# Second group's second layer partly in three passes, half of the h tiles scaled in place in PSUM, and another order of the w_out parts

## The chip, the cores and the metric

One Trainium2 chip, of which one core is used. A core has a tensor engine (PE; its weight loads are shown apart, as PEld), a vector engine (DVE), a scalar engine (ACT), a gpsimd engine (POOL) and a sync engine (SP), which here issues every DMA in program order. The metric is the device time of one execution in microseconds (us); times are the median of several runs. Each engine runs its own queue of instructions in order and waits on semaphores where it needs another engine's result. PSUM, into which PE writes, has eight banks here, all handed out from one pool.

## The reference

A gated linear attention feeds a two-layer network. q, k, v and alpha have 4 batches, 8 heads, 768 steps and 48 channels.

```
for t in range(S):
    state = alpha[t][:, None] * state + outer(k[t], v[t])     # 48 x 48 per head
    y[t] = q[t] @ state
x = y with batch and step as 3072 rows, head and channel as 384 columns
h = maximum(x @ w_in, 0)          # w_in 384 x 2048
out = (h * h) @ w_out             # w_out 2048 x 384, out 3072 x 384 in fp32
```

w_in and w_out arrive as 64-bit floats and are turned into fp32 on DVE and ACT at the start.

## The kernel before, in words

**Tiles.** The sequence is cut into chunks of 128 steps: 6 chunks times 4 batches are 24 blocks. Four blocks, one chunk of all batches, are a group of 512 tokens; there are 6 groups, 0 to 5. The hidden size of 2048 is 16 tiles of h, each 128 x 512 (hidden channels by the group's tokens). Each weight matrix is cut into 8 pieces of 128 x 768, two tiles of h each.

**Order.** The program is written under a manual schedule: each engine runs its instructions in the order in which the Python code gives them. The attention of group g + 1 is woven into the network of group g. `weave` (L885) walks a list of units of the network, each with a cost (one unit is about 1.3 us of PE), and ahead of each unit it puts the events whose position has come. Events are attention steps, preparation of weights, splits of x, and loads. Their positions stand in the dictionary `AT` (L19) and in `PLAN` and `EARLY`.

**Two ways to multiply.** A plain fp32 product runs as two records on PE. In the other way, three passes in the faster fp32r type, each factor is split into a rounded part and a rest: `cast_w` (L561) makes b of a weight piece on ACT, `rest_w` (L565) the rest l on DVE, `scale_w` (L569) scales l by 1/E on ACT (E is 2^-12), and `diff_w` (L574) makes d, the difference of b and l, on DVE. `split_to` and `diff_to` make a, l and d of x or h: a on ACT (L600), l on DVE (L559), d on DVE (L604). A product is then E times the sum of b·a and l·l, plus d·d. The l and d parts of all pieces are stored to DRAM by `scale_w` and `diff_w` and loaded back into SBUF when room comes free: `pump` (L589) issues the next load of a list as long as fewer than `room` parts are held, and `stream(g)` puts the next group's list there at unit 26. The tiles for weights come from one pool of 25 (`wt_pool`).

**Groups.** Group 0 computes both layers plain (`ffn_in` L758, `ffn_out` L778 with its products at L783). Group 1 computes layer 1 in three passes and layer 2 plain. Groups 2 to 5 use three passes in both. While group 1 runs, the rest of w_in (pieces 4 to 7) and all of w_out are prepared for the groups behind it.

**Layer 1 in three passes** (`layer_in`). `in_x` (L634) gives the b·a and l·l products of an h tile (L626), and ACT copies the bank to an SBUF tile with the factor E (L639). Two tiles later `in_y` (L641) gives the d·d products in the same bank, and DVE adds them to the SBUF tile (L559). At `AT["post"]`, four tiles later, `in_post` (L645) takes max(h, 0) squared: odd tiles in one DVE operation (L648), even tiles in two ACT operations (L652, L653).

**Layer 2 in three passes** (`layer_out`). A first sweep over the 16 tiles, `out_x` (L697), adds the a·b and l·l products of four token tiles into four banks (L692); ACT copies them to SBUF with E. A second sweep, `out_y` (L714), adds the d·d products, DVE adds the two, and the rows are stored. `split_h` and `diff_h` make the parts of h ahead of that.

**Attention, per block.** Logarithms of alpha are summed along the chunk by a product with a triangular matrix, `cs` (L273). Blocks below `SPLIT`, 8, do it in one plain product (L278); others have their logarithms split on DVE (`sp`, L269 and L270) and use two fp32r products (L281, L282). Exponentials of the sums scale q and k; `turn` (L486) transposes both into two banks (L494); `ga` and `gb` then give scores (L389), sums of k times v for each half of the chunk (`state_sums`, L406, products L413), the new state (`sums_copied` L420, `next_state` L427 on DVE) and y (L365). The k·v sums are 64 columns wide, of which 16 are a neighbouring head's and are not used.

Of the kernel before, what the change touches and what calls it, by code (L numbers as in the profile page):

```python
# [18 lines left out]
AT = {'evs': 0.8, 'lead': 4, 'post': 4, 'w_first': (40, 44, 48, 52), 'wstep': 1, 'w_in_at': 2, 'w_in_by': 3.4, 'w_out_at': 27, 'w_out_by': 3.6, 'room1': 6, 'room': 9, 's0': 2, 'ahead': 5, 'late': 1, 'xs': 0.5, 'g1': (2.7, 20, 32.0), 'g': (1.2, 15.5), 'g1x': 48, 'gx': 46, 'g0x': 55.5, 'pre': 0, 'ga': 9, 'gb': 12}  # L19

# [6 lines left out]
def kernel(  # L27
# [10 lines left out]

# [27 lines left out]
    s_t = [p2.tile([128, NP, 64], FP32, tag="s", name="s", bufs=B + 2) for _ in range(B)]  # L78
    for t in s_t:
        nc.gpsimd.memset(t, 0.0)  # L80
    NV = 4
# [8 lines left out]
    wt_pool = ctx.enter_context(tc.tile_pool(name="wt", bufs=25))  # L90
# [13 lines left out]

# [39 lines left out]


# [75 lines left out]
    for i in range(2):  # L221
        rows = slice(64 * i, 64 * (i + 1))
        nc.gpsimd.tensor_copy(out=halves_mask[rows], in_=causal[rows, rows])
    last = consts.tile([128, 4, NP], FP32, name="last")
# [36 lines left out]
    SPLIT = 2 * GB  # L261
# [113 lines left out]

# [27 lines left out]
    def state_sums(n):  # L406
        ps = two[n]
        for p in range(NP):
            for e in range(2):
                first = (2 * p + e) * D - G * e  # L410

                for h in range(1 if n // B == NCH - 1 else 2):
                    nc.tensor.matmul(  # L413
                        out=ps[h][64 * e : 64 * (e + 1), 1, p, :],
                        lhsT=tile_of("k", n)[HALF[h], 2 * p + e, :],
                        rhs=tiles["v"][n % NV][HALF[h], first : first + 64],
                        start=True, stop=True, skip_group_check=True,
                    )

    def sums_copied(n):  # L420

        ps = two.pop(n)
        u = blk[n]["u"] = p2.tile([128, NP, 64], FP32, tag="us", name="us", bufs=3)
        nc.vector.tensor_tensor(out=u, in0=ps[0][:, 1], in1=s_t[n % B], op=ALU.add)
        blk[n]["kv1"] = ps[1][:, 1]

    def next_state(n):  # L427
        blk[n]["s"] = s_t[n % B]
        if n // B < NCH - 1:
            s = s_t[n % B] = p2.tile([128, NP, 64], FP32, tag="s", name="s", bufs=B + 2)  # L430
            last = last_t[n % 4].unsqueeze(2).to_broadcast([128, NP, 64])
            nc.vector.tensor_tensor(out=s, in0=blk[n].pop("kv1"), in1=blk[n]["u"], op=ALU.add)
            nc.vector.tensor_tensor(out=s, in0=s, in1=last, op=ALU.mult)
# [18 lines left out]
    def ga(a, n):  # L452

        if n is not None:
            for f in (scores, state_sums, masked, sums_copied):
                f(n)
        if a is not None:
            product = y_begin(a)
            for h in range(1 if a < B else 0, 2):
                for m, p, e in heads(a):  # L460
                    rows = slice(64 * e, 64 * e + D)
                    s = blk[m]["u" if h else "s"]
                    product(m, p, e, s[rows, p, 0 : D + G * e], blk[m]["qs"][rows, p, HALF[h]], HALF[h])


            for m, p, e in heads(a):
                end = inner(product, m, p, e, e)
            passed = nc.gpsimd.nop(nofuse=True)
            dep(passed, end)
            two["y"] = product, passed  # L470
        if n is not None:
            next_state(n)
# [79 lines left out]
    here, todo, room = {}, [], [6]  # L552
# [11 lines left out]

    def rest_w(w, p):  # L565
        l = here["l", w, p] = wt("wl", FP32R, shapes[w])
        combine(((l, whole[w][p], ALU.subtract, here["b", w, p].bitcast(FP32)),))

    def scale_w(w, p):  # L569
        l = here["l", w, p]  # L570
        nc.scalar.activation(out=l, in_=l.bitcast(FP32), func=AF.Copy, scale=1.0 / E)
        nc.sync.dma_start(out=kept_parts["l", w, p], in_=words(l))

    def diff_w(w, p):  # L574
        b, l = (here[x, w, p].bitcast(FP32) for x in "bl")
        d = here["d", w, p] = wt("wd", FP32R, shapes[w])
        combine(((d, b, ALU.subtract, l),))
        nc.sync.dma_start(out=kept_parts["d", w, p], in_=words(d))
        if w == "o":
            here.pop(("l", w, p))  # L580
            here.pop(("d", w, p))
            pump()
# [6 lines left out]
    def pump():  # L589
        while todo and sum(k[0] in "ld" for k in here) < room[0]:  # L590
            key = todo.pop(0)
            here[key] = wt("w" + key[0], FP32R, shapes[key[1]])
            nc.sync.dma_start(out=words(here[key]), in_=kept_parts[key])
# [40 lines left out]
    def in_x(j):  # L634
# [3 lines left out]
        hid[j] = two_k("hid")  # L638
        nc.scalar.activation(out=hid[j], in_=acc["h", j], func=AF.Copy, scale=E)  # L639

    def in_y(j):  # L641
        in_passes(j, "d", "d", False, True)
        combine(((hid[j], acc.pop(("h", j)), ALU.add, hid[j]),))

    def in_post(j):  # L645
        h = hid[j]
        if j % 2:
            nc.vector.scalar_tensor_tensor(  # L648
                out=h, in0=h, scalar=0.0, in1=h, op0=ALU.max, op1=ALU.mult
            )  # L650
        else:
            nc.scalar.activation(out=h, in_=h, func=AF.Relu)  # L652
# [5 lines left out]
    def layer_in(g):  # L658
        units = []
        for n in range(NJ + 2):  # L660
# [6 lines left out]
            if g > 1 and AT["lead"] <= n < AT["lead"] + AHEAD:  # L667
                units.append((0, split_h, (n - AT["lead"],)))
                units.append((0, diff_h, (n - AT["lead"],)))
# [5 lines left out]
    def split_h(n):  # L675
        r = n % (AHEAD + MORE)
        if r < AHEAD:
            a, l = two_k("ha", FP32R), two_k("hl", FP32R)
        else:
            if n < AHEAD + MORE and r == AHEAD:  # L680
                extra[:] = [raw_r("hx") for _ in range(3)]
            i = 2 * (r - AHEAD)
            a, l = (extra[i // 3][:, i % 3] for i in (i, i + 1))
# [6 lines left out]

    def of_tile(t, lhs, rhs, start=False, stop=False):
# [5 lines left out]
    def out_x(n):  # L697
        p, jj = divmod(n, 2)
        a, l = h_parts.pop(n)
        for t in range(GB):  # L700
            if n == 0:
                acc[t] = ps_ffn.tile([128, GB * C], FP32, tag="att", name="o")
            of_tile(t, a, here["b", "o", p][:, jj], start=n == 0)
            of_tile(t, l, here["l", "o", p][:, jj], stop=n == NJ - 1)
            if n == NJ - 1:
                if t % 2 == 0:
                    acc["out", t // 2] = cv_pool.tile([128, 2, DM], FP32, tag="upper", name="osb")
                nc.scalar.activation(
                    out=acc["out", t // 2][:, t % 2, :], in_=acc[t][:, 0:DM], func=AF.Copy, scale=E
                )  # L710
# [3 lines left out]
    def out_y(g, ps, t, last):  # L714
        for p in ps:
            for jj in range(2):
                of_tile(
                    t, h_diff[2 * p + jj], here["d", "o", p][:, jj],
                    stop=last and (p, jj) == (ps[-1], 1),
                )  # L720
        if last:
            o = acc["out", t // 2][:, t % 2, :]
# [8 lines left out]
    def layer_out(g):  # L731
        posts = list(range(NJ + 2 - AT["post"], NJ))
        units = []
        if g == 1:
            units += plain_out(g)
            for i, n in enumerate(posts):
                units.insert(1 + 2 * i, (0, in_post, (n,)))
            return units
        ahead, late = AT["ahead"], AT["late"]
        split = [f for n in range(AHEAD, NJ) for f in ((0, split_h, (n,)), (0, diff_h, (n,)))]  # L740
        for _ in range(AT["s0"]):
            units += [split.pop(0), split.pop(0)]
        for i in range(NJ):
            units.append((1.08, out_x, (i,)))
            if posts:
                units.append((0, in_post, (posts.pop(0),)))
            done = (len(split) + 1) // 2
            while split and NJ - (len(split) + 1) // 2 <= i + ahead and (
                split[0][1] is diff_h or split[0][2][0] - AHEAD - MORE <= i
            ):  # L750
                units += [split.pop(0), split.pop(0)]
        ps = list(range(NW))
        steps = [ps] if g == NG - 1 else [ps[i : i + 2] for i in range(0, NW, 2)]
# [43 lines left out]


# [26 lines left out]


# [24 lines left out]
    def attention(pairs, scale):  # L851
# [3 lines left out]
        for t, n0, after, *last in pairs:  # L855
            for at, fs in EARLY if n0 < SPLIT else PLAN:
                for f in fs.split():
# [4 lines left out]
                    if f == "gb" and after:  # L862
                        for p in range(NP):
                            out.append((w + 0.8 * p, ev_part, (n0 - 2, p)))
# [39 lines left out]
    units += plain_out(0)  # L904
# [5 lines left out]
    events += attention([(0, GB, False), (18.0, GB + 2, True), (27.5, GB + 4, True, True)], 2.35)  # L910
    events += splits_of_x(AT["g0x"], 1)
    weave(units, sorted(events, key=lambda x: x[0]))
    hid.clear()

    def stream(g):
# [6 lines left out]
        todo.extend(keys + [(x, "o", p) for x in "ld" for p in range(NW)])  # L922
        pump()

    for g in range(1, NG):
        events = []
        if g + 1 < NG:
            n = GB * (g + 1) + 2
            if g == 1:
                t0, t1, t2 = AT["g1"]  # L930
                pairs = [(t0, n - 2, False), (t1, n, True), (t2, n + 2, True)]
            else:
                t0, t1 = AT["g"]
                pairs = [(t0, n, True), (t1, n + 2, True)]
            events += attention(pairs, 1)
            events += splits_of_x(AT["g1x" if g == 1 else "gx"], g + 1)
        if g == 1:
            for p in range(NW // 2, NW):
                events += prepare(AT["w_in_at"] + AT["w_in_by"] * (p - NW // 2), "i", p)
            for p in range(NW):  # L940
                events += prepare(AT["w_out_at"] + AT["w_out_by"] * p, "o", p)
# [38 lines left out]
```

## Time and profile before

| | |
|---|---|
| median of 3 runs | 529.47 us (528.05 to 529.89) |
| profiled execution | 528.17 us, its span 526.4 us |
| granted PE clock, mean | 0.999 |
| group 1, layer 1 | 129.7 to 168.0 us |
| group 1, layer 2 | 168.0 to 222.6 us |
| group 2 | 222.6 to 302.0 us |
| group 3 | 302.0 to 381.5 us |
| group 4 | 381.5 to 456.7 us |
| group 5 | 456.7 us to the end |

The stages are read off the chain of waits, where the lines of PE's products change: L626 is layer 1 in three passes, L692 layer 2 in three passes, L763 and L783 the plain layers. All work of a stage, the woven attention included, lies in its stretch. The profile is of one execution; the span runs from its first to its last instruction, and what the device time has beyond it lies around the program.

### The profile page before, as it was taken

The numbers are of one execution on the slowest core, as the hardware profiler recorded it, in microseconds if no ns is written. First come the engines' busy times: TensorE is split into PE (matmuls) and PEld (weight loads), VectorE is DVE, ScalarE is ACT, GpSimd is POOL, SyncE is SP. The second block draws the span as 40 slices with busy tenths as digits, with TensorE's granted clock in tenths as the row PEclk, the third lists the DMA queues.
The fourth block names the chain that finished last, engine by engine and source line by source line (L and its number), as shares of the span: only waits on it lengthen the run. The fifth ranks groups of instructions, "written<-read, shape, count | busy, mean of one in ns | idle before, by whom it ended". The sixth has DMA issues, their size and how long they took to land.

```text
span 526.4 us, 12821 instructions
## 1 busy us (share of the span) xinstructions
PE 517.0 (98%) x5228; PEld 411.4 (78%) x5228; DVE 361.7 (69%) x615; ACT 319.1 (61%) x654; POOL 4.1 (1%) x24
## 2 busy tenths in 40 slices
PE   8989999999999999999999999999999999999997
PEld 5754455666887666688899988899988899988996
DVE  4798979973788465667698457788456587456861
ACT  4668875666877485576963366964366874156620
POOL 3000000000000000000000000000000000000000
PEclk9999999999999999999999999999999999999999
DMA  9999667373375786498974797964773544898301
GB/s 162 208 271 266 154 207 193 78 223 121 114 192 153 222 226 184 177 309 192 225 199 139 230 281 180 235 178 143 219 257 126 180 151 136 279 331 283 112 2 60
DMA packets 140130, 99.98 MB, mean 190 GB/s; under 512 B 111380, under 2 KB 114472, under 8 KB 140072
## 3 DMA queue, kind: packets, MB, share of 16 engines
q1 hardware_dynamic: 140072, 99.17, 67.1%
q8 instruction: 41, 0.67, 0.5%
q14 instruction: 17, 0.14, 0.1%
HBM read 81.82 MB, written 17.33 MB: 188 GB/s over the span
## 4 chain that ended last, share of the span: by engine, by line
PE 93%; DMA 3%; DVE 1%; ACT 1%; SPq 1%; POOL 1%; issue 0%; POOLq 0%; DVEq 0%
PE h L626 32%; PE o L692 25%; PE o L783 16%; PE h L763 7%; PE y L365 4%; PE T L494 2%; PE sckv L389 2%; PE sckv L413 2%; PE cs L278 1%; DMA a_lent<-in_alpha_dram 1%; DMA a_in<-in_alpha_dram 1%; DMA row<-b 1%; DVE x L527 1%; PE cs L281 1%; PE cs L282 1%
## 5 line engine op out<-in xcount | busy, mean ns | idle before, releaser
L639 ACT ACTIVATE hid<-h 128x512 f32<-128x512 f32 x80 | 47.1, 593 | 71.5 <-PE h L626 71.3
L783 PE MATMUL o<-w_out,hid 128*128 128x384 f32 x256 | 86.3, 491 | 0.7 <-issue 0.7
L559 DVE TENSOR_TENSOR hid<-h,hid 128x512 f32<-128x512 f32 x80 | 54.5, 687 | 42.1 <-PE h L626 38.4
L783 PEld LDWEIGHTS o<-w_out,hid 128*128 128x128 f32 x256 | 47.6, 190 | 32.6 <-issue 1.6
L626 PE MATMUL h<-xa,wb 128*128 128x512 f32 x240 | 68.5, 394 | 0.0
L626 PE MATMUL h<-xd,wd 128*128 128x512 f32 x240 | 68.5, 398 | 0.0
L626 PE MATMUL h<-xl,wl 128*128 128x512 f32 x240 | 67.7, 390 | 0.0
L527 ACT COPY x<-y 32x256 f32<-32x256 f32 (+2 forms) x132 | 46.9, 365 | 29.4 <-PE y L365 23.7
L626 PEld LDWEIGHTS h<-xl,wl 128*128 128x128 f32 x240 | 45.0, 188 | 9.7
L626 PEld LDWEIGHTS h<-xa,wb 128*128 128x128 f32 x240 | 44.9, 188 | 9.8
L626 PEld LDWEIGHTS h<-xd,wd 128*128 128x128 f32 x240 | 43.8, 188 | 9.2
L692 PE MATMUL o<-wd,hd 128*128 128x384 f32 x256 | 45.0, 334 | 0.0
L763 PE MATMUL h<-x,w_in 128*128 128x512 f32 (+1 forms) x108 | 43.5, 550 | 1.2 <-ACT x L527 1.2
L692 PEld LDWEIGHTS o<-wd,hd 128*128 128x128 f32 x256 | 44.4, 188 | 0.0
L692 PE MATMUL o<-wb,hx 128*128 128x384 f32 x128 | 43.1, 337 | 0.0
L692 PE MATMUL o<-wl,hl 128*128 128x384 f32 x128 | 42.8, 334 | 0.0
L692 PE MATMUL o<-wb,ha 128*128 128x384 f32 x128 | 42.8, 334 | 0.0
L692 PE MATMUL o<-wl,hx 128*128 128x384 f32 x128 | 42.8, 334 | 0.0
L763 PEld LDWEIGHTS h<-x,w_in 128*128 128x128 f32 x108 | 20.0, 190 | 21.3 <-issue 16.7
L397 DVE COPY_PREDICATED am<-halves_mask,sckv 128x256 f32<-128x256 uint32 x48 | 18.6, 440 | 15.4 <-PE sckv L413 14.9
L600 ACT ACTIVATE ha<-hid 128x512 fp32r<-128x512 f32 x32 | 20.1, 631 | 14.9 <-PE o L692 5.2
L559 DVE TENSOR_TENSOR hl<-hid,ha 128x512 fp32r<-128x512 f32 x32 | 22.0, 689 | 8.0 <-ACT ha L600 7.9
(109 smaller groups left out, 826.1 us busy)
## 6 DMA issues: line engine op xcount, KB each, us to landing
wl<-li SPq DMA_DIRECT2D x32, 384.0 KB
wd<-di SPq DMA_DIRECT2D x32, 384.0 KB
wl<-lo SPq DMA_DIRECT2D x32, 384.0 KB
wd<-do SPq DMA_DIRECT2D x32, 384.0 KB
raw<-in_moe_w_in_dram SPq DMA_DIRECT2D x8, 768.0 KB
raw<-in_moe_w_out_dram SPq DMA_DIRECT2D x8, 768.0 KB
v_in<-in_v_dram SPq DMA_DIRECT2D x24, 192.0 KB
out_dram<-osb SPq DMA_DIRECT2D x24, 192.0 KB
```

The lines of the kernel that those rows point to most:

```text
L365: ins = nc.tensor.matmul(out=ys[e][64 * half : 64 * half + D + G * e, m % 2, p // 2, t], lhsT=lhsT, rhs=rhs, start=(half, e) not in seen, ...
L389: nc.tensor.matmul(out=ps[e][HALF[h], 0, p, :], lhsT=ks[rows, p, HALF[h]], rhs=qs[rows, p, HALF[h]], start=True, stop=True, skip_group_che ...
L397: nc.vector.copy_predicated(out=am_h(n)[:, e, n % 2], data=ps[e][:, 0], mask=halves_mask.bitcast(U32).unsqueeze(1).to_broadcast([128, NP, ...
L413: nc.tensor.matmul(out=ps[h][64 * e : 64 * (e + 1), 1, p, :], lhsT=tile_of("k", n)[HALF[h], 2 * p + e, :], rhs=tiles["v"][n % NV][HALF[h], ...
L527: copy(out=x[kk][to : to + m, t : t + 2], in_=blk[n]["y"][e][r : r + m, :, p // 2],)
L559: nc.vector.tensor_tensor(out=o, in0=x, in1=z, op=op)
L600: nc.scalar.activation(out=a, in_=x, func=AF.Copy, scale=NEAR)
L626: nc.tensor.matmul(out=acc["h", j], lhsT=here[w, "i", p][:, kk, jj * 128 : (jj + 1) * 128], rhs=x_parts[x][:, kk], start=start and kk == 0 ...
L639: nc.scalar.activation(out=hid[j], in_=acc["h", j], func=AF.Copy, scale=E)
L692: nc.tensor.matmul(out=acc[t][:, 0:DM], lhsT=lhs[:, t * C : (t + 1) * C], rhs=rhs, start=start, stop=stop, skip_group_check=True,)
L763: nc.tensor.matmul(out=ps, lhsT=w[:, kk, c0 : c0 + 128], rhs=xT[g][kk][:, cols], start=(kk == 0), stop=(kk == KM - 1),)
L783: nc.tensor.matmul(out=acc[t][:, 0:DM], lhsT=hid[per * i + j][:, t * C : (t + 1) * C], rhs=w_out[i][:, j, :], start=(i == 0 and j == 0), s ...
```

## The change

**Group 1's second layer.** Its first three pieces of w_out (`k1` is 5, so 8 − 5) stay plain (`out_plain`), and ACT copies their sums to SBUF. The last five pieces, ten tiles of h, go through `out_x` and `out_y`. Where `out_x` ends, DVE now adds E times the bank to the plain sum.

**Half of the h tiles in place.** A string gives each tile, by its number modulo 4, a kind: ADAD in group 1, ADMD behind it. D is what it was, with the DVE square. For A and M, ACT scales the bank in place in PSUM, the d·d products are added on top of it, and ACT takes the maximum with zero from the bank to SBUF; then the square is taken on ACT (A) or DVE (M). The DVE addition falls away for these tiles. `post` is 3, not 4.

**Weights.** The parts of w_out are prepared in the order 3, 4, 5, 6, 7, 0, 1, 2: piece 3 in group 0 at unit 52, the others in group 1 at units 16, 24, 20, 26, 30, 37 and 38. Pieces 3 to 7 keep their l in SBUF; their d is stored and loaded again for group 1 (five more loads of 384 KB), by an event at unit 25.5. The pool of weight tiles has 26 instead of 25, and `pump` counts all parts held against a room of 23 or 25. A piece's four steps stand 1.6 units apart instead of 1.

**Attention.** `SPLIT` is 12, so blocks 8 to 11 use the plain sum. The k·v sums and the states are computed on the 48 columns that are used (`own`), in tiles that are set to zero once. Positions of the steps in `AT` are changed for every group.

```diff
-AT = {'evs': 0.8, 'lead': 4, 'post': 4, 'w_first': (40, 44, 48, 52), 'wstep': 1, 'w_in_at': 2, 'w_in_by': 3.4, 'w_out_at': 27, 'w_out_by': 3.6, 'room1': 6, 'room': 9, 's0': 2, 'ahead': 5, 'late': 1, 'xs': 0.5, 'g1': (2.7, 20, 32.0), 'g': (1.2, 15.5), 'g1x': 48, 'gx': 46, 'g0x': 55.5, 'pre': 0, 'ga': 9, 'gb': 12}
+AT = {'evs': 0.4, 'lead': 4, 'post': 3, 'w_first': (43, 45, 47, 49), 'wstep': 1.6, 'w_in_at': 2, 'w_in_by': 3, 'room1': 23, 'room': 25, 's0': 4, 'ahead': 5, 'late': 2, 'xs': 0.2, 'g0': (-0.5, 19.5, 27.5), 'sc0': (2.35, 2.35, 2.35), 'g1': (0.5, 17.0, 30.5), 'g': (2.2, 15.0), 'g1x': 51, 'gx': 47, 'g0x': 54.5, 'k0': 0, 'h0': 16, 'k1': 5, 'h1': 4, 'h1by': 4, 'evs0': 0.3, 'tp': 'ADMD', 'tp1': 'ADAD', 'split': 12, 'o0': (52,), 'o1': (16, 24), 'o2': (20, 26, 30, 37, 38), 'str1': 25.5, 'ga': 9, 'gb': 12.5}
...
-    wt_pool = ctx.enter_context(tc.tile_pool(name="wt", bufs=25))
+    wt_pool = ctx.enter_context(tc.tile_pool(name="wt", bufs=26))
...
-    SPLIT = 2 * GB
+    SPLIT = AT["split"]
...
-                first = (2 * p + e) * D - G * e
+                first = (2 * p + e) * D
...
-                        out=ps[h][64 * e : 64 * (e + 1), 1, p, :],
+                        out=ps[h][64 * e : 64 * (e + 1), 1, p, G:64],
                         lhsT=tile_of("k", n)[HALF[h], 2 * p + e, :],
-                        rhs=tiles["v"][n % NV][HALF[h], first : first + 64],
+                        rhs=tiles["v"][n % NV][HALF[h], first : first + D],
...
     def diff_w(w, p):
-        b, l = (here[x, w, p].bitcast(FP32) for x in "bl")
-        d = here["d", w, p] = wt("wd", FP32R, shapes[w])
+        b, l = here["b", w, p].bitcast(FP32), made["l", w, p].bitcast(FP32)
+        d = made["d", w, p] = wt("wd", FP32R, shapes[w])
+        cut.add((w, p))
         combine(((d, b, ALU.subtract, l),))
-        nc.sync.dma_start(out=kept_parts["d", w, p], in_=words(d))
-        if w == "o":
-            here.pop(("l", w, p))
-            here.pop(("d", w, p))
-            pump()
+        keep("d", w, p)
+        for x in "ld":
+            t = made.pop((x, w, p))
+            if w == "i" or p >= NW - AT["k0"] or (x == "l" and p >= NW - AT["k1"]):
+                here[x, w, p] = t
+        pump()
...
     def pump():
-        while todo and sum(k[0] in "ld" for k in here) < room[0]:
+        while todo and todo[0] in stored and len(here) + len(made) + 2 * NW - len(cut) < room[0]:
...
     def in_x(j):
...
-        hid[j] = two_k("hid")
-        nc.scalar.activation(out=hid[j], in_=acc["h", j], func=AF.Copy, scale=E)
+        x = acc["h", j]
+        if kinds[0][j % 4] == "D":
+            hid[j] = two_k("hid")
+            nc.scalar.activation(out=hid[j], in_=x, func=AF.Copy, scale=E)
+        else:
+            nc.scalar.activation(out=x, in_=x, func=AF.Copy, scale=1.0 + E)
 
     def in_y(j):
         in_passes(j, "d", "d", False, True)
-        combine(((hid[j], acc.pop(("h", j)), ALU.add, hid[j]),))
+        if kinds[0][j % 4] == "D":
+            combine(((hid[j], acc.pop(("h", j)), ALU.add, hid[j]),))
...
     def in_post(j):
...
+        h = hid[j] = two_k("hid")
+        nc.scalar.activation(out=h, in_=acc.pop(("h", j)), func=AF.Relu)
+        if kinds[0][j % 4] == "M":
+            combine(((h, h, ALU.mult, h),))
         else:
-            nc.scalar.activation(out=h, in_=h, func=AF.Relu)
             nc.scalar.activation(out=h, in_=h, func=AF.Square)
...
+    def out_plain(p, t, pieces):
+        if p == 0:
+            new_sum(t)
+        for n in (2 * p, 2 * p + 1):
+            of_tile(t, hid[n], w_out[p][:, n % 2], start=n == 0, stop=n == 2 * pieces - 1)
+        if p == pieces - 1:
+            nc.scalar.activation(out=new_out(t), in_=acc.pop(t)[:, 0:DM], func=AF.Copy)
...
             if n == NJ - 1:
...
+                x = acc[t][:, 0:DM]
+                if first:
+                    o = out_tile(t)
+                    nc.vector.scalar_tensor_tensor(
+                        out=o, in0=x, scalar=E, in1=o, op0=ALU.mult, op1=ALU.add
+                    )
+                else:
+                    nc.scalar.activation(out=new_out(t), in_=x, func=AF.Copy, scale=E)
...
     def layer_out(g):
...
+        plain = NW - AT["k0"] if g == 0 else NW - AT["k1"] if g == 1 else 0
+        first = 2 * plain
+        units = [(1, out_plain, (p, t, plain)) for p in range(plain) for t in range(GB)]
...
+            for i in range(min(AHEAD, len(split) // 2)):
+                units[at:at] = split[0:2]
+                del split[0:2]
+                at += 2 + AT["h1by"]
...
         if g == 1:
-            for p in range(NW // 2, NW):
-                events += prepare(AT["w_in_at"] + AT["w_in_by"] * (p - NW // 2), "i", p)
-            for p in range(NW):
-                events += prepare(AT["w_out_at"] + AT["w_out_by"] * p, "o", p)
+            m = len(AT["w_first"])
+            for p in range(m, NW):
+                events += prepare(AT["w_in_at"] + AT["w_in_by"] * (p - m), "i", p)
+            for i, at in enumerate(AT["o1"] + AT["o2"]):
+                events += prepare(at, "o", order[len(AT["o0"]) + i])
+            n = min(AT["k0"], AT["k1"])
+            todo.extend(("l", "o", p) for p in range(NW - n, NW))
+            events.append((AT["str1"], stream_out, (AT["k1"], "d")))
```

## The prediction

> **What bounds the kernel now.** I read the page's head first, then its chain by engine, then the chain of waits in order of time, and last the windows of group 1's two layers.
>
> ```profile
> span 526.4 us, 12821 instructions
> PE 517.0 (98%) x5228; PEld 411.4 (78%) x5228; DVE 361.7 (69%) x615; ACT 319.1 (61%) x654; POOL 4.1 (1%) x24
> PE 93%; DMA 3%; DVE 1%; ACT 1%; SPq 1%; POOL 1%; issue 0%; POOLq 0%; DVEq 0%
> ```
>
> TensorE is busy for 98% of the span and carries 93% of the chain. The chain in order of time shows no gap on it from 35.4 to 168.0 us and from 222.6 to 489.4; its idle time lies in the opening (2.9 us before 18, 2.0 up to 35.4), in 0.74 us at 179.8, and in some 3.7 us after 489.4. So a change that shortens TensorE's work shortens the kernel, as long as the other engines still deliver in time. The unit prices come from the same chain:
>
> ```profile
> 48.36 0.65 PE cs L278 x2
> ...
> 136.60 0.18 PE cs L281
> 136.95 0.18 PE cs L281
> 137.13 0.18 PE cs L282
> 137.31 5.48 PE h L626 x24
> ...
> 204.73 0.47 PE sckv L389 x32
> 205.20 0.47 PE sckv L413 x32
> 205.66 16.97 PE o L783 x52
> ...
> 489.43 33.32 PE o L692 x192
> ```
>
> A record of a plain product in layer 2 takes 16.97/52 = 0.326 us, and a plain product is two records (L783 has 256 of them for 128 products): 0.653. A record of the three passes takes 33.32/192 = 0.1735, three of them 0.521. A plain sum over a block (cs) takes 0.65. In hi and lo parts, two blocks run from 136.60 to 137.31 (one record is missing there): 0.71, or 0.355 a block.
>
> What stands beside TensorE in group 1, layer 1 and then layer 2:
>
> ```profile
> 129.70:168.00 38.30, 38.30 (x314) 31.38 (x313) 30.25 (x54) 29.62 (x58) 0.00 (x0) 1.00 0.57 148
> 168.00:222.60 54.60, 53.86 (x710) 34.46 (x709) 33.32 (x57) 33.14 (x72) 0.00 (x0) 1.00 0.71 203
> ```
>
> Columns: stretch, its us, busy us of PE, PEld, DVE, ACT and POOL, PE clock, DMA share, GB/s. In layer 2 DVE and ACT are each busy for some 33 of 54.6 us. That is the spare room the change spends.
>
> **TensorE's own work.** Compared queue by queue, the changed program has 88 plain products in layer 2 where there were 128, and 120 more pass records. So 10 tiles of h times 4 token tiles change over: 40 × (0.653 − 0.521) = **−5.3 us**, all on the chain.
>
> Here a rule speaks against the exchange. The Trainium skill, "Perfetto Trace Analysis", section "Identifying the Most-Contended Engine", holds matmul busy for a bad measure and tells one to look at weight-load busy instead. Two windows, passes in group 2 and plain products in group 1:
>
> ```profile
> 273.00:301.00 28.00, 28.00 (x164) 28.00 (x163) 1.00 0.61 182
> 206.00:222.00 16.00, 16.00 (x51) 9.48 (x50) 1.00 0.53 170
> ```
>
> Weight loads fill the passes completely (28.00 of 28.00) and only 9.48 of 16.00 us of the plain products. By that measure 120 pass loads of 0.17 us (20.8) replace 80 plain ones of 0.19 (15.2), a loss of 5.6 us. But an instruction stream costs what lies between its starts, and that is 0.326 and 0.1735 a record. I take −5.3.
>
> Blocks 8 to 11 get the plain sum (all four in group 1's layer 1): 4 × (0.65 − 0.355) = **+1.2 us**.
>
> The state sums (L413) move 48 instead of 64 columns. 32 of them take 0.47 us, 14.7 ns each; there are 704, and four blocks' worth lie in the opening, where TensorE is not the bound, which leaves 18 blocks' worth on the chain. By columns that is 0.47/4 × 18 = −2.1. The rule in "TensorEngine Tiling (Array Packing)", "Performance Considerations", gives such a product a fixed cost of about 60 cycles and the same time for any shorter free size: 60/64 of 0.47 saves 0.029 a block, −0.5. The nearest rows are the scores (L389), which move 64 columns and also take 0.47, and no row here has fewer columns, so it shows neither. The weight loads, 64 columns, stay what they are, which speaks for the small gain. I take **−0.5**, ends 0 and −2.1.
>
> **Vector and scalar work in group 1's layer 2.** This is where cover may run out. TensorE's stage shrinks from 54.6 to 49.3.
>
> ```profile
> L639 ACT ACTIVATE hid<-h 128x512 f32<-128x512 f32 x80 | 47.1, 593 | 71.5 <-PE h L626 71.3
> L559 DVE TENSOR_TENSOR hl<-hid,ha 128x512 fp32r<-128x512 f32 x32 | 22.0, 689 | 8.0 <-ACT ha L600 7.9
> ```
>
> DVE gains two operations (hl, hd) for each of 10 tiles. The row says 689 ns, but one follows the other after 0.60 to 0.64, so 10 × 2 × 0.64 = 12.8. The sum of the plain and the pass half of the output adds 8 short operations of about 0.5: 4.0. Preparing w_out starts earlier, which moves about 5 weight operations of 0.91 out of the stage: −4.5. So 33.3 becomes 45.6 of 49.3, 92%. ACT gains 10 × 0.6 to about 39 of 49.3. It has room.
>
> Walking DVE's queue through the stage, each h tile's difference is needed only in the second sweep, and the first tile's split begins some units ahead of its products. What waits in TensorE's order is: the transposes of k and q behind the products with b and 1/b (slack below 0.6 us), the four output sums ahead of the last sweep (0 to 1.2 us late), and the d parts of pieces 5, 6 and 7. These last are loaded back through SP's queue, in which they stand behind the stores of the differences of w_out pieces 1 and 2, which DVE makes late. Behind them again stand the first l and d parts of group 2. Five loads more make about 12.3 MB in 49.3 us, 250 GB/s, where slices of this trace reach 309 to 331. I put **+1.0** for all of it, ends 0 and +7.7 (see the slower rival).
>
> **Groups 2 to 5.** Half of the h tiles no longer pass through an SBUF copy and a DVE add: TensorE adds the d products on the scaled bank itself. In all, 40 DVE adds of 0.62 go, 16 DVE squares come and 16 ACT squares go. Both engines get lighter and neither is the bound. What can get later is the bank: Relu reads it now and frees it about one unit (1.3 us) later, and the second transpose bank waits for such a one. The posts come one unit earlier, and the walk leaves 1.4 us. In-place scaling is not in this trace; it would have to take over 2 us instead of L639's 0.593 to delay the d products, which stand two tiles behind. 0, at worst +2. The state updates on DVE shrink to 48 columns; five memsets are added on POOL (busy 4.1 of 526.4), behind the masks that TensorE's first product at 4.35 us waits for; 0. In group 0 the preparation of one w_out piece (two ACT and two DVE operations, two stores on SP) joins L783's run at about 120 us, where ACT and DVE have nothing due before group 1; 0, at worst the 0.9 of one operation before the parts of x.
>
> The attention steps move by up to 3 units in all groups, with the loads they issue on SP. Their work is the same, and in a pair's order (exponentials, products with q and k, transposes, scores) nothing passes another, so they only meet other tiles of layer 1: 0, and the bank wait above is the price if not.
>
> **Sum.** −5.3 + 1.2 − 0.5 + 1.0 = −3.6. The profiled execution took 528.17 us (span 526.4), so 524.6. It lies 1.3 below the median of 529.47; from the median, 525.9. I take 525.2. Its own range is 523.5 to 527.5.
>
> **Rivals.**
>
> *Columns count, nothing stalls:* −5.3 + 1.2 − 2.1 = −6.2, 522.0 (523.3 from the median). For it: no stall in 222.6 to 489.4 in a similar pass layer. Against it: 92% on DVE.
>
> *Slower: DVE's queue is the bound of group 1's layer 2.* The waits in that stage, with total, times and longest:
>
> ```profile
> DVE wl L559 <- DMA lo<-wl: 4.1, 3, 1.6
> DVE s L433 <- DMA last<-row: 3.8, 1, 3.8
> DVE wd L559 <- ACT wl L571: 3.0, 2, 2.1
> DVE wl L559 <- ACT wb L563: 2.5, 1, 2.5
> ```
>
> That is 13.4 us in which DVE waits for something other than TensorE. If they all stay, 45.6 + 13.4 = 59.0. The last 4.0 (output adds, the differences of x) may run over, so TensorE stands for 59.0 − 4.0 − 49.3 = 5.7; the last differences and the stores behind them then also hold up the first l part of group 2, 384 KB at 250 GB/s = 1.6 and its issue, about 2.0. Together 7.7: −5.3 + 1.2 − 0.5 + 7.7 = +3.1, 531.3. It decides once the waits left exceed 7.7 us, and the gain is gone at a stall of 4.6, so at 10 to 12 us of waits. Against it: wl's wait for its old tile's store goes as l parts stay in SBUF, and preparation is spread wider (1.6 units a step, not 1), so wb and wl should be ready.
>
> *Only the reloads are late:* group 2 starts, or the last sweep waits, 3 us more: about 528 (527.6), no change.
>
> That the exchange does not happen is out: the queues hold the counts given above.
>
> **Chances.** Likeliest case 0.49, columns 0.17, no change 0.14, slower 0.20. A difference below 0.3% (1.6 us) cannot be told from none here. Faster: 0.49 + 0.17 = 0.66; same 0.14; slower 0.20. The range, 521.5 to 531, takes in the columns case and most of the slower one.
>
> **What will show it.** Group 1's layer 2 near 50.3 us instead of 54.6, its layer 1 near 39.5; 32 state sums at 0.44 rather than 0.35; DVE near 45 us in that stage, with waits below 5; TensorE without gaps in groups 2 to 5. I am wrong if TensorE shows stalls above 4 us between 168 and 225 that end on DVE or a load of d parts, or new ones before transposes in groups 2 to 5.

## The result

| | before | changed |
|---|---|---|
| median | 529.55 us (528.05 to 529.89, 4 runs) | 524.52 us (524.29 to 525.34, 4 runs) |
| ratio, with 95% interval | | 0.9916 (0.9894 to 0.9937) |
| profiled execution, span | 528.17, 526.4 | 524.45, 522.7 |

The changed kernel is faster by 0.6 to 1.1%; 525.2 was forecast. The head of the profile after, its chain by engine and the two groups that were shown of before:

```profile
span 522.7 us, 12883 instructions
PE 514.0 (98%) x5268; PEld 418.0 (80%) x5268; DVE 355.4 (68%) x611; ACT 312.7 (60%) x648; POOL 5.3 (1%) x29
PE 93%; DVE 2%; DMA 2%; SPq 1%; issue 1%; ACT 0%; DVEq 0%
L639 ACT ACTIVATE h<-h 128x512 f32<-128x512 f32 x40 | 23.3, 581 | 61.2 <-PE h L622 61.2
L547 DVE TENSOR_TENSOR hl<-hid,ha 128x512 fp32r<-128x512 f32 x38 | 26.1, 687 | 7.5 <-ACT ha L596 7.5
```

TensorE is still 98% busy and still the chain, with more records (5268, 5228 before) in 3 us less. Scaling a bank in place takes ACT 581 ns, as the copy to SBUF did (593). Group 1's layers 1 and 2 in the windows view, with the columns of the prediction:

```profile
130.46:171.28 40.82, 40.82 (x345) 32.46 (x345) 27.67 (x46) 34.21 (x70) 0.00 (x0) 1.00 0.68 186
171.28:218.53 47.25, 47.25 (x718) 39.24 (x717) 40.90 (x75) 31.79 (x70) 0.00 (x0) 1.00 0.78 208
```

Layer 1 is 2.5 us longer, layer 2 is 7.4 us shorter, and in neither does TensorE stand still. What moved between them is seen in the chains in order of time, two lines of before and then the kernel after:

```profile
170.59 1.15 PE T L494 x32
...
179.81 0.74 issue
```

```profile
134.56 0.65 PE cs L265 x2
135.20 0.69 PE h L622 x3
135.90 0.65 PE cs L265 x2
...
161.03 0.64 PE cs L265 x2
161.68 1.39 PE h L622 x6
163.07 0.65 PE cs L265 x2
163.71 4.12 PE h L622 x18
167.84 1.15 PE T L482 x32
168.99 2.29 PE h L622 x9
171.28 1.29 PE o L701 x4
172.58 0.62 PE sckv L372 x32
173.20 0.45 PE sckv L395 x32
...
205.85 12.68 PE o L701 x72
218.53 4.12 PE h L622 x18
222.66 0.13 issue
```

Four plain sums of 0.65 now stand in layer 1. So does one run of transposes (T, 1.15 us) that stood in layer 2 before, and 1.15 us of the shift between the layers is its own. Pass records still come every 12.68/72 = 0.176 us. By stage, from the starts of the first products of each in the two chains, in us:

```
                    before    after   difference
opening              35.42    36.27     +0.85
group 0              94.32    94.19     -0.13
group 1, layer 1     38.27    40.82     +2.55
group 1, layer 2     54.62    47.25     -7.37
group 2              79.35    80.25     +0.90
group 3              79.58    79.21     -0.37
group 4, 5, tail    144.84   144.71     -0.13
span                526.40   522.70     -3.70
```

The opening ended between 35.2 and 37.0 us in the profiles of eleven further executions below, nearly all of them with the same opening, so its 0.85 says nothing of the change. Without it the change is worth 4.55 us between the profiles (490.98 and 486.43), which is near the 5.0 between the medians.

### The profile page after: what moved, and what is told of

Same layout as the page of the kernel before. It is cut to its first block, busy times and chain, and to the rows that moved or that the text cites. A ratio compares the mean times of both kernels' runs of the same rounds, so it can differ in the third digit from the quotient of the medians.

```text
span 522.7 us, 12883 instructions
## 1 busy us (share of the span) xinstructions
PE 514.0 (98%) x5268; PEld 418.0 (80%) x5268; DVE 355.4 (68%) x611; ACT 312.7 (60%) x648; POOL 5.3 (1%) x29
## 4 chain that ended last, share of the span: by engine, by line
PE 93%; DVE 2%; DMA 2%; SPq 1%; issue 1%; ACT 0%; DVEq 0%
PE o L701 33%; PE h L622 32%; PE o L825 8%; PE h L805 7%; PE y L352 4%; PE T L482 2%; PE sckv L372 2%; PE sckv L395 2%; PE cs L265 2%; DMA qk_lent<-in_q_dram 1%; SPq L303 1%; SPq L109 1%; DMA a_in<-in_alpha_dram 1%; DVE x L515 0%; PE cs L268 0%
## 5 line engine op out<-in xcount | busy, mean ns | idle before, releaser
L547 DVE TENSOR_TENSOR hid<-h,hid 128x512 f32<-128x512 f32 x40 | 27.6, 689 | 55.2 <-PE h L622 51.4
L639 ACT ACTIVATE h<-h 128x512 f32<-128x512 f32 x40 | 23.3, 581 | 61.2 <-PE h L622 61.2
L701 PE MATMUL o<-wd,hd 128*128 128x384 f32 x296 | 52.1, 334 | 0.0
L701 PEld LDWEIGHTS o<-wd,hd 128*128 128x128 f32 x296 | 51.4, 188 | 0.0
L701 PE MATMUL o<-wb,ha 128*128 128x384 f32 x152 | 50.9, 335 | 0.0
L701 PE MATMUL o<-wl,hl 128*128 128x384 f32 x152 | 50.9, 335 | 0.0
L701 PE MATMUL o<-wb,hx 128*128 128x384 f32 x144 | 48.7, 338 | 0.0
L825 PE MATMUL o<-w_out,hid 128*128 128x384 f32 x128 | 42.8, 490 | 0.0
L637 ACT ACTIVATE hid<-h 128x512 f32<-128x512 f32 x40 | 23.9, 599 | 27.8 <-PE h L622 27.7
L825 PEld LDWEIGHTS o<-w_out,hid 128*128 128x128 f32 x128 | 23.9, 190 | 16.0
```

Source lines behind the costliest of these rows:

```text
L547: nc.vector.tensor_tensor(out=o, in0=x, in1=z, op=op)
L637: nc.scalar.activation(out=hid[j], in_=x, func=AF.Copy, scale=E)
L639: nc.scalar.activation(out=x, in_=x, func=AF.Copy, scale=1.0 + E)
L701: nc.tensor.matmul(out=acc[t][:, 0:DM], lhsT=lhs[:, t * C : (t + 1) * C], rhs=rhs, start=start, stop=stop, skip_group_check=True,)
L825: nc.tensor.matmul(out=acc[t][:, 0:DM], lhsT=hid[per * i + j][:, t * C : (t + 1) * C], rhs=w_out[i][:, j, :], start=(i == 0 and j == 0), s ...
```

## The experiments

Twelve kernels ran. All but one start from the changed kernel, and their times stand against its 524.5. They ran at other times than it; the median of the kernel before, run beside each of them, lay between 528.9 and 529.7, so a difference of a few tenths between two kernels says nothing.

**Take the exchange away.** All eight pieces plain.

```diff
-'k1': 5, 'room1': 23
+'k1': 0, 'room1': 18
```

> The changed kernel with group 1's second layer all plain (eight pieces, no passes; the room for parts is 18 so that the tiles fit). If the gain is the 40 exchanged products, PE's work grows by 40 x 0.132 = 5.3 us and the time goes from 524.5 to 529.8, all of it in group 1's layer 2 (47.3 to 52.6 us). If the gain came from the new positions of the attention, or from lighter DVE and ACT, it stays within 2 us of 524.5.

Measured 532.98 us (530.28 to 534.74), 8.5 more instead of 5.3. TensorE's waits between 36 and 490 us, with total, times and longest, in this kernel:

```profile
PE h L622 <- issue: 1.2, 1, 1.2
PE y L352 <- issue: 1.1, 2, 0.7
PE h L622 <- DMA wd<-di: 1.1, 1, 1.1
```

They sum to 3.4 us, where the changed kernel has 0.3. From group 1's layer 2 to the end of group 3's layer 1 this kernel takes 180.38 us and the changed one 171.65. Of the 8.73, 3.1 are added waits, and 5.6 is left for the 40 products. The positions of the attention and the lighter DVE and ACT were kept in this run, so they are not the gain: the exchange is. Of the rest, 1.1 us is the price of a queue that was not arranged for the plain layer: group 2's first d part (wd<-di) came behind the four output stores, for which SP stood up to 11.9 us until ACT had copied the sums. The others are gaps without a releaser, to which the last section returns.

**Take single parts away.** The plain sums (`'split': 12` to `8`), the narrow state sums, and the kinds A and M of h tile. A tile of kind D brings back the addition on DVE, and it also has its square taken on DVE: for a tile of kind A both are new there, and the kernel before had ACT square half of its tiles.

```diff
-ps[h][64 * e : 64 * (e + 1), 1, p, G:64]   with rhs columns first : first + D
+ps[h][64 * e : 64 * (e + 1), 1, p, :]      with rhs columns first - G * e, 64 of them
...
-'tp': 'ADMD', 'tp1': 'ADAD'
+'tp': 'DDDD', 'tp1': 'DDDD'     (all_d)
+'tp': 'DDDD', 'tp1': 'ADAD'     (d_in_2_to_5)
```

> The changed kernel with blocks 8 to 11 back on two fp32r products for their sums. If the plain sums are a pure loss on PE, group 1's layer 1 gets 1.2 us shorter and the time is 523.3. If DVE needs the room that the eight hi and lo operations (about 4.4 us) take, PE stalls behind the sums or the transposes in group 1 and the time is 524.5 or more.

> The changed kernel with the state sums and states on 64 columns again. If columns set the cost of these products, 32 of them go from 0.35 to 0.47 us and the time to 526.6; if a fixed cost per product does, they go from 0.45 to 0.47 and the time to 524.8 at most.

> The changed kernel with every h tile of kind D: the copy to SBUF with E and DVE's addition again for 40 tiles, 24.8 us more of DVE and none less of ACT. If scaling in place is worth nothing on the path, the time stays at 524.5 (within 1.6). If the new positions (the square three tiles behind, the shorter layer 2) need it, PE stalls in groups 1 to 5 by 2 us or more, in waits for DVE or for a bank.

> The changed kernel with the in-place tiles kept in group 1 (ADAD) and every tile of groups 2 to 5 of kind D. All tiles of kind D lost 3.7 us in group 1's layer 1, where the chain ran along DVE, and nothing visible behind it. If scaling in place pays in group 1 alone, the time is 524.5, within 1 us; if it also pays in groups 2 to 5, it is above 526.

| | median | range, runs |
|---|---|---|
| split8 | 524.90 | 524.65 to 525.46, 4 |
| kv64 | 524.81 | 524.26 to 526.31, 5 |
| all_d | 528.50 | 526.13 to 530.28, 12 |
| d_in_2_to_5 | 524.93 | 524.12 to 526.10, 6 |

*split8.* The 1.2 us do not come back. Layer 1 did get shorter, from 40.82 to 39.89:

```profile
129.38:169.27 39.89, 39.83 (x345) 32.43 (x345) 30.71 (x54) 34.30 (x70) 0.00 (x0) 1.00 0.70 192
```

DVE has 30.7 us of work there instead of 27.7, and the chain leaves TensorE for ACT and DVE between 161.3 and 166.5 us. Then the profile loses it again: from the start of group 1's layer 2 to the end of group 2's layer 1 it takes 94.32 us instead of 92.44. Of that, TensorE stands for 2.0 us instead of 0.4, and 1.4 of it is one "issue" gap, of which more below. So the plain sums cost 1.2 us on TensorE and cost nothing net in the runs; that DVE's room is the whole reason is not shown, since the gap is not DVE's.

*kv64.* 0.3 us, inside the ranges, and not 2.1, so the columns do not set the price of these products. In the changed kernel's chain 32 records of 48 columns take 0.45 or 0.46 us, where 64 columns took 0.47.

*all_d and d_in_2_to_5.* In groups 2 to 5 kind D costs nothing that can be told (0.4 us, inside the ranges), and in group 1 it costs 3.6 us, what is left of the 4.0. There layer 1 takes 44.55 us instead of 40.82. The windows of layer 1 and of its end, and TensorE's waits, in the kernel with every tile of kind D:

```profile
131.19:175.74 44.55, 42.81 (x346) 33.66 (x345) 36.23 (x61) 29.65 (x59) 0.00 (x0) 0.97 0.67 179
170.00:176.00 6.00, 5.12 (x34) 3.88 (x33) 5.51 (x10) 4.49 (x11) 0.00 (x0) 0.72 0.70 166
PE T L482 <- DVE q_in L284: 1.7, 2, 0.9
```

DVE is busy for 36.2 us instead of 27.7, and ACT for 29.7 instead of 34.2. Of DVE's 15 further operations in the layer, eight are additions and seven are squares. Over the whole span DVE's additions go from 40 to 80 and its squares from 56 to 80. The changed kernel's additions, and then both groups with every tile of kind D:

```profile
L547 DVE TENSOR_TENSOR hid<-h,hid 128x512 f32<-128x512 f32 x40 | 27.6, 689 | 55.2 <-PE h L622 51.4
L547 DVE TENSOR_TENSOR hid<-h,hid 128x512 f32<-128x512 f32 x80 | 55.0, 687 | 39.3 <-PE h L622 38.3
L651 DVE SCALAR_TENSOR_TENSOR hid<-hid 128x512 f32<-128x512 f32 x80 | 54.5, 681 | 0.0
```

In all DVE has 37.5 us more and ACT 33.3 less, where the expectation had 24.8 more and none less. So the run undoes two things, the scaling in place and ACT's share of the squares, and it does not show which of them group 1 needs. A kernel that adds on DVE again and squares half of the tiles on ACT, as before, was not run.

How DVE holds TensorE up is in the trace. Transposes wait for the products of q on DVE, twice and some 0.9 us each, and then the granted clock is at half. Idle 1.7 and some 1.5 us lost to the clock up to the layer's end make most of the 3.7. The second half of the layer is the tight one: 150 to 170 us had DVE busy for 18.24 of 20, and 15.31 in the changed kernel.

**More and fewer pieces in passes.**

```diff
-'k1': 5, 'room1': 23
+'k1': 4, 'room1': 22     (four_pieces)
+'k1': 6, 'room1': 24     (six_pieces)
+'k1': 7, 'room1': 25     (seven_pieces)
+'k1': 6, 'room1': 24, 'h1': 2, 'h1by': 1 instead of 4 and 4     (six_early)
```

> Four pieces in passes, four plain (room 22). PE has 8 products of three passes fewer and 8 plain ones more: +1.1 us against the changed kernel, 525.6, with no stall, and group 1's layer 2 at 48.3 us. If the changed kernel already pays for late splits in its fifth piece, the time falls below 524.5.

> The changed kernel with six of eight pieces in passes (two plain; room 24). PE's work shrinks by 8 x 0.132 = 1.1 us. In the profile of the changed kernel DVE is busy for 40.9 of 47.3 us in group 1's layer 2; two tiles more add 2.5, so 43.4 of 46.2, and if that room is usable the time is 523.4. If DVE or a reload is already the bound, PE stalls by 1 us or more and the time is 524.5 or above.

> Seven of eight pieces in passes (room 25). PE's work shrinks by 2.1 us against the changed kernel, to 45.2 in group 1's layer 2; DVE has 40.9 + 5.0 = 45.9 us of work there. DVE becomes the bound: a stall of 1 to 4 us and a time of 523.5 to 526.5. If DVE is not what bounds, 522.4.

> Six pieces in passes, with the splits of the first three of their h tiles moved ahead: they stand behind units 2, 5 and 8 of the plain part instead of 4, 10 and its end. In the run with six pieces the chain left PE between 179.7 and 198.4 us: one split of ten was made before the pass sweep, the next nine followed in a burst, and the products of k and q behind it held up a transpose for 3.8 us. If the order of the queues made that stall, most of it goes and the time is 523.4 to 526. If DVE and ACT have no room left for six pieces in any order, it stays above 529.

Four 529.59 us (526.88 to 530.77), six 531.50, seven 532.42, six early 531.88. Every neighbour of five loses 5 to 8 us, and moving three splits ahead did not help. What holds TensorE up in the run with six is a wait of 3.8 us of the transposes for the product of k with 1/b. DVE's timeline, first in the changed kernel, with its line, operation, tiles and start:

```profile
187.23 0.68 DVE L547 TENSOR_TENSOR hl<-hid,ha 128x512 fp32r<-128x512 f32 x1
187.95 0.69 DVE L600 SCALAR_TENSOR_TENSOR hd<-ha,hl 128x512 fp32r<-128x512 f32 x1
188.56 0.55 DVE L284 TENSOR_TENSOR k_in<-k_in,inv 128x384 f32<-128x384 f32 x1
```

and in the run with six pieces:

```profile
191.47 0.69 DVE L547 TENSOR_TENSOR hx<-hid,hx 128x512 fp32r<-128x512 f32 x1
...
196.39 0.69 DVE L600 SCALAR_TENSOR_TENSOR hd<-hx 128x512 fp32r<-128x512 f32 x1
197.00 0.55 DVE L284 TENSOR_TENSOR k_in<-k_in,inv 128x384 f32<-128x384 f32 x1
```

The splits that open the pass sweep follow each other on DVE. With twelve plain units ahead of them this burst stands behind the third attention pair's products of k and q; with eight it stands ahead of them, and so ahead of the transposes. The sum of the losses fits: 1.1 us of products less, 5.6 of added waits and 2.2 of half clock while TensorE works make 6.7 of the 7.0 us. DVE's load over the stage does not explain it, since it is busy for 41.0 of 55.1 us there, and for 40.9 of 47.3 in the changed kernel. That the order is the cause is argued and not shown. The run with three splits moved up was to test it, and by its own expectation its time speaks for engines that have no room in any order. Its trace leaves both open: eight operations of the burst still stand from 190.85 to 196.3 ahead of the same product, which is late by the same 3.8 us, but DVE had just stood 3.4 us for ACT's first part, and ACT was busy for 4.8 of the 5 us from 185 to 190 (4.9 in the changed kernel). Whether six pieces pay with that attention pair moved, or with less on ACT, was not tried.

Four pieces lose at the other end, at a load of d parts. TensorE's waits, and SP's queue with what each entry moves:

```profile
PE o L701 <- DMA wd<-do: 2.3, 1, 2.3
```

```profile
208.53 1.19 SPq L556 DMA_DIRECT2D do<-wd  x2
209.81 0.42 SPq L589 DMA_DIRECT2D wd<-do  x1
210.32 1.48 SPq L109 DMA_DIRECT2D v_in<-in_v_dram  x2
211.89 1.54 SPq L109 DMA_DIRECT2D k_in<-in_k_dram  x1
213.48 0.69 SPq L589 DMA_DIRECT2D wd<-do  x1
```

SP stood 6.4 us for DVE's difference (wd) before it could store it at 208.53. The last d load came behind v and k, at 213.48, where the changed kernel issues its last two at 209.27. One plain piece more also leaves one tile of room less, so the run changes two things. So whether the late store or the smaller room made that load late is not told apart. The products that waited lost 2.3 us, and the clock did the rest:

```profile
216.00:218.00 2.00, 0.43 (x3) 0.11 (x1) 1.89 (x4) 0.00 (x0) 0.00 (x0) 1.00 0.98 365
218.00:220.00 2.00, 1.26 (x5) 1.26 (x6) 0.56 (x1) 0.00 (x0) 0.00 (x0) 0.81 1.05 398
220.00:222.00 2.00, 2.00 (x7) 2.00 (x7) 0.60 (x2) 0.00 (x0) 0.00 (x0) 0.50 0.70 269
222.00:224.00 2.00, 2.00 (x10) 1.78 (x10) 1.07 (x2) 0.00 (x0) 0.00 (x0) 0.84 0.58 212
```

The sixth of the numbers after the stretch, ahead of the last two, is the granted clock. After the pause it falls to 0.50 and is full again by 224: 2 × (0.19 + 0.50 + 0.16) = 1.7 us lost while TensorE works. 1.1 for the piece, 2.3 and 1.7 make the 5.1.

With seven pieces a sum over a block waits 4.4 us for its hi part on DVE, behind a like burst.

**POOL takes the splitting of the logarithms.**

```diff
-'split': 12
+'split': 8     (split8_pool; in pool_sums blocks 0 to 3, 8 and 9 take the plain sum)
...
-        nc.vector.tensor_copy(out=hi, in_=la)
-        nc.vector.tensor_tensor(out=lo, in0=la, ...)
+        nc.gpsimd.tensor_copy(out=hi, in_=la)
+        nc.gpsimd.tensor_tensor(out=lo, in0=la, ...)
```

> The changed kernel with blocks 8 to 11 on two fp32r products, and with the hi and lo parts of the logarithms made on POOL instead of DVE for all blocks that need them. If only DVE's queue ate the 1.2 us that PE gained in the run with the split at 8, they now show: 523.3, with group 1's layer 1 at 39.6 us and layer 2 at 47.3. If POOL is too slow (more than about 4 us for a pair of blocks) the sums are late and PE stalls in every group: above 526.

> A version meant to be faster than both. The changed kernel with the hi and lo parts made on POOL for all blocks that use them, and with blocks 4 to 7, 10 and 11 moved from the plain sum to two fp32r products (blocks 0 to 3, 8 and 9 stay plain, because POOL's 3.4 us for a pair came too late for 8 and 9 in the run with the split at 8 on POOL). PE's work shrinks by 6 x 0.295 = 1.8 us, from 524.5 to 522.7, 1.2 in group 0 and 0.6 in group 1's layer 1. If POOL's queue, or blocks 4 to 7's exponentials behind it, are late, PE stalls in group 0 and the time is 524.5 or more.

With the split at 8, 524.07 us (522.46 to 527.05): between the two expectations, and not told from the changed kernel. With the sums of blocks 4 to 7, 10 and 11 in two parts, 526.86 (524.84 to 530.94), slower than the 522.7 expected and than the changed kernel. TensorE came to the transposes at 88.1 us instead of 89.8, 1.7 earlier, and then waited 1.2 us for q, after which the clock fell to 0.50 again. DVE's product with q was 1.9 us later than in the changed kernel. The groups of DVE from 36 to 92 us show where DVE lost time; the changed kernel:

```profile
L157 DVE TENSOR_SCALAR upper<-raw 128x768 uint32<-128x768 uint32 x11 | 6.1, 556 | 0.0
```

and this one:

```profile
L157 DVE TENSOR_SCALAR upper<-raw 128x768 uint32<-128x768 uint32 x11 | 8.5, 771 | 0.0
```

The same operation is 215 ns longer on average. The longest, 1.35 us, began at 41.58, beside a subtraction on POOL that began at 41.33. POOL's casts, 0.50 us elsewhere, took up to 1.27. That this lengthening made q late is likely and was not tested by itself.

**The kernel before, once more.**

> The kernel before, unchanged, for a second profile. The medians differ by 5.1 us and the two profiled executions by 3.7. If the first profile of it caught a short execution, another one is near 529.5 and shows in its stages where the 1.4 us are: in the opening, if the loads' landing varies; in groups 2 to 5, if a stall of PE there comes and goes, of which the changed kernel is free.

Its profiled execution took 528.72 us, its eight runs a median of 529.19. Its stages differ from the first profile's by 0.35 us at most: a gap of 0.39 us in group 3, and 0.2 in the opening. The stall of over a microsecond in groups 2 to 5 that the expectation thought of is not there. From the end of the opening on, the two profiles of before take 490.98 and 491.27 us and the changed one 486.43. That is 4.6 and 4.8 us of the 5.0 between the medians; the rest is in executions of which there is no profile, and stays open.

## Why the prediction was right, point by point

**The exchange, −5.3.** Right. Layer 2 lost 7.37 us; 1.15 of it is the run of transposes that went to layer 1, and 0.74 the "issue" gap at 179.8 that did not come back. That leaves 5.5. Taking the exchange away gave 5.6. The record spacing was the right measure. Weight-load busy rose by 6.6 us over the whole span (411.4 to 418.0) while the time fell. The Trainium skill's "Perfetto Trace Analysis" ("Identifying the Most-Contended Engine") has weight-load busy, beside the share of peak arithmetic, tell how near a kernel is to the limit; taken as the price of an exchange, as the prediction tried it, it has the wrong sign here.

**The plain sums, +1.2.** Right as TensorE time (four times 0.65 in layer 1), wrong as a loss of the change: undoing them gained nothing in the medians. What took the 1.2 back is not settled.

**The state sums, −0.5.** Right side, half the size: 18 × 0.015 = 0.27 from the records, and the run on 64 columns agrees with it inside its range. The fixed cost in the Trainium skill's "TensorEngine Tiling (Array Packing)" ("Performance Considerations"), by an estimate from which 32 products take 60/64 of 0.47 or 0.44 us, comes much nearer to the measured 0.45 than the columns do, with 0.35.

**Stalls, +1.0.** Mis-sized. In layer 2 TensorE did not stand at all, and group 2 lost some 0.4 us in two gaps. DVE was busy for 40.9 us and not 45.6: three of its products with q and k went to layer 1, the state updates got shorter (358 ns for 425), and the output sums cost 3.5 and not 4.0. Its waits for anything but TensorE came to 2.2 us; 13.4 had been kept in the slower rival. The transfers were too large in the sum as well: 208 GB/s over layer 2, or 9.8 MB, where 12.3 MB and 250 GB/s were put.

**The slower rival** did not happen, but it had the place right. Its two mechanisms, a DVE queue that is late for TensorE and d loads behind stores that wait for DVE's differences, are seen in the kernels with six and four pieces. DVE's sum in the stage does not tell when they bite: the forecast compared 59.0 with 49.3, and the run with four pieces has less DVE work than the changed kernel.

**In-place tiles: "0, at worst +2".** This step missed. The prediction priced them in groups 2 to 5, where 0 was right. In group 1's layer 1, into which part of the preparation of w_out was moved, kind A covers 3.7 us: so much longer was the layer with every tile of kind D. The prediction counted about five weight operations out of layer 2 (−4.5 us) and did not ask what they would meet in layer 1. A part that costs nothing by itself can thus be the cover for another. Whether the addition that falls away or the square that stays on ACT is the cover is open.

**The sum** of −3.6 against −3.7 between the spans is in part luck. Without the opening's +0.85 the profiles differ by 4.55, about 1 us more than the forecast. The "issue" gap that did not come back (−0.74) was in no term, and the stalls were 0.4 instead of 1.0. The mechanism, the exchange at the price of the records, was right.

## What to carry to other kernels

Where one engine is full, price an exchange on it by the spacing of its records, and then ask of each helper engine, stage by stage, what its queue holds *ahead of* the next thing the full engine waits for; a stage's sum of busy time does not tell that. A removal that looks free may be the cover for a move elsewhere in the same change, so price the two together. And a stall of a full TensorE can cost more than its own length: in six of these kernels the clock then stood at half for 3.4 us, which is 1.7 us lost where TensorE works all that time, and in two of the six for twice as long.

## What the runs showed of the hardware that was not expected

**The clock after short pauses.** The granted clock fell to 0.50 after one pause of 2.3 us (four pieces), after two of 0.9 among transposes (every tile of kind D), and after two of 0.4 and 0.9 among transposes (the POOL version):

```profile
88.00:90.00 2.00, 1.49 (x25) 1.01 (x24) 2.00 (x5) 0.16 (x1) 0.00 (x0) 1.00 0.88 315
90.00:92.00 2.00, 1.20 (x9) 0.98 (x10) 1.93 (x4) 1.58 (x2) 0.00 (x0) 0.72 0.87 241
92.00:94.00 2.00, 2.00 (x4) 1.01 (x3) 1.97 (x3) 0.00 (x0) 0.00 (x0) 0.50 0.65 104
```

By windows of half a microsecond it stood at half for 3.4 us in these three and in the run with seven pieces (a pause of 4.4), and for 6.8 in the two runs with six (3.8). The gap of 0.74 in the kernel before, gaps of 1.1 and 1.2 with every piece plain and one of 1.4 in split8 left it at 1.00, so length alone does not decide. The Trainium skill's "TensorE: Matmul & The Clock Gate" ("HAM oscillation") warns of idle gaps above about 3.4 us; by that figure those up to 2.3 us would have cost their own length alone. Here they were enough. What decides between 1.2 us in two waits, which brought half clock, and 1.4 in one, which did not, is not shown.

**Gaps with nothing to wait for.** TensorE paused 0.3 to 1.4 us in group 2's y products (260 to 268 us) in most runs of the changed kernel and its variants, and 0.74 and 0.77 at 180 us in both profiles of the kernel before, in every case with no releaser in the profile. In four profiles a packet of the instruction queue began one to three microseconds ahead, and over the six to eight us around the gap the data queue held 73 to 86% of the DMA engines. Such packets come about every 13 us, so this suggests late instructions and does not show it.

**DVE and POOL beside each other.** One-input DVE operations went from 0.55 to as much as 1.35 us beside POOL's casts and subtractions. The Trainium skill's "SBUF — State Buffer" ("SBUF: two separate sides") tells of a port pair that one of the two holds for a whole instruction; a lengthening by 0.8 us, where POOL's operations take 0.5 and 1.0 alone, agrees with it.
